# A 32x32 triangular solve by two 16x16 triangles and tensor products, in the first two of six attention blocks

## The chip, the cores and the metric

The kernel runs on one core of a Trainium2 chip. The metric is the device time of one execution in microseconds (us). Before the change it is 2233.88 us, the median of three runs (2229.7, 2233.88 and 2234.07). A core has a tensor engine (TensorE, PE in the profile), a vector engine (VectorE, DVE), a scalar engine (ScalarE, ACT), a general engine (GpSimd, POOL) and one that issues DMAs here (SyncE, SP). Each works through its own instructions in order, and waits for the others by semaphores.

## The reference

Three layers follow each other. The first is linear attention with the delta rule, one state per batch and head:

```
k_n = k / (norm(k) + 1e-6)
for t in range(768):
    y[t]  = q[t] @ state
    state = state + beta[t] * outer(k_n[t], v[t] - state^T k_n[t])
```

There are 4 batches of 8 heads, 768 tokens and a head size of 48. The second layer is `(h * tanh(softplus(h))) @ w_out` with `h = x @ w_in`, over 3072 tokens, model size 384 and inner size 2048. The third has a gate that is normalised eight times over rows and columns (all tokens enter every column sum), and eight experts of inner size 1024, whose outputs are added with the gate's weights.

## The kernel before

The attention is computed by chunks of 64 tokens, two chunks to a block, six blocks. Inside a chunk the token loop becomes a unit lower triangular system, one per batch, head and chunk: 64 systems of 64x64 in a block. The matrix is the masked product of the keys with themselves (tile `gx`, written by `st_g` and `mask_g`). A system is cut in two triangles of 32x32 and a square. `lane_in_one` transposes `gx` in 32x32 squares, so that each partition of tile `lane` holds one 32x32 triangle, with 1 on its diagonal. `elim_ops` inverts all of them by 30 steps on VectorE; a step multiplies a row into a column (into scratch in `t11`) and adds it (60 operations in all, L1083 and L1089). `st_lane_out` transposes the result back into `t11` (L1098) and into `diag`, which lies in tile `yd` (L1099). Then TensorE forms the square's part: `st_m1` (L1126, on `t11`), `st_place`, `st_m2` (L1141, on `diag`). After that come the block's chain of stages: `st_w` (L1190), `st_s` (L1208, L1209), `st_z` (L1168, L1169), `st_y` (L1224), each with a pass of VectorE or ScalarE behind it, and `st_x1`, which turns the block's output for the second layer.

Block 0 stands alone at the start (the prologue): nothing else for TensorE is there but the keys' products of block 1 (`st_g(1, ...)`, L1020 and L1021, raw values that ScalarE copies out; GpSimd masks them later) and the masked products of queries and keys (`gq`, L1006, four pairs of VectorE operations). Block 1's elimination begins there with 18 operations on GpSimd (`elim1`).

Window 0 follows: 16 steps of the second layer on block 0's tokens. A step `f` does `m_first(f)` on TensorE (nine products, L300), Mish on ScalarE, `gl` on VectorE (L1299), and two steps later `m_second(f)` (nine products, L1310). In window 0 the weights also come in and are split into parts: `begin_decode`, three integer passes on VectorE (L189, L192, L197) and one more (L262), after ScalarE's conversions (L206, L260). Steps with the experts follow in the same window (`hl` and L324). Beside the steps a table, `PLACES`, names the marks (s0 to s15, f1 to f4, s16 to s23) at which the next block's stages are put in: the first number `m0` is the mark at which what is left of the elimination is drained and transposed back; the list behind it places the chain. `fill(x)` hands out waiting elimination operations worth x us by the planner's own cost at the end of each step. So the order of every engine is fixed when the program is built.

Of the kernel before, what the change touches and what calls it, by code (L numbers as in the profile page):

```python
# [84 lines left out]
def delta_mish_sinkhorn_kernel(  # L85
# [240 lines left out]


    gate = const.tile([128, 192], F32, name="gate")
    sk = {}
    for name, at, cols in (("ones", 0, 128), ("m", 128, 3), ("cs", 136, E), ("cr", 144, E), ("rs", 152, NT)):  # L330
        sk[name] = gate[:, at:at + cols]
# [445 lines left out]
    def o_store():  # L777

        u, half, t = todo.popleft()
        if t < 0:  # L780
            f, x, (n, d) = fin[u], slice(512 * half, 512 * half + 512), divmod(~t, KD)
            tt(out=f[:, d, x], in0=f[:, d, x], in1=f[:, 3 + 3 * n + d, x], op=ALU.add)
            return
            return True
        o_write(u, half, t, o_turn(u, half, t, (0, 1, 2)))

    todo = deque()
# [8 lines left out]
    if True:  # L796
# [9 lines left out]
        lane = ap_p.tile([128, 32, 32], F32, name="lane")  # L806
# [268 lines left out]
        def elim_ops(c, eng=(nc.vector,)):  # L1075
            ops = []
            for s in range(1, 31):
                n = 31 - s
                slot = [None]

                def prod(s=s, n=n, slot=slot):
                    slot[0] = t11.rearrange("p b i -> p (b i)")[:, 0:n * s].rearrange("p (n s) -> p n s", s=s)
                    eng[0].tensor_tensor(  # L1083
                        out=slot[0], in0=lane[:, s + 1:32, s:s + 1].to_broadcast([128, n, s]),
                        in1=lane[:, s:s + 1, 0:s].to_broadcast([128, n, s]), op=ALU.mult,
                    )
# [8 lines left out]
            return ops  # L1095

        def st_lane_out(c):
            nc.vector.transpose(out=t11.rearrange("p b i -> p i b"), in_=lane.rearrange("p t i -> p i t"))  # L1098
# [258 lines left out]
        with tc.manual_schedule():  # L1357
# [44 lines left out]
            for _, op in lane_in_one(0):  # L1402
                op()
            e0 = [op for _, op in elim_ops(0)]

            def el(n):
                for _ in range(n):
# [10 lines left out]
            banks[:] = [0, [A1, A1, (ps_o1, "o0")]]  # L1418
            for t in range(4):
                run(*[lambda hf=hf: st_g(1, t, hf, False) for hf in range(2)])  # L1420
            for n in range(4):
                begin_decode(n)
            el(len(e0) - 24)
            nc.vector.memset(mi_f[1][:, 0:1], 0.0)
            warm(12, i=1)
            el(len(e0))
            st_lane_out(0)

# [1 line left out]
                for _ in range(n):  # L1430
                    dq.popleft()[1]()

            def elim1(n, eng):
                elim_eng[0] = eng
                for _ in range(min(n, len(ops1))):
                    ops1.popleft()[1]()

            m1a = m_run(st_m1(0, 0, (32,)))
            m1a[0]()
            st_place(0, 0, (0, 2))  # L1440
# [2 lines left out]
            m2a()  # L1443
            m1b()
            wa = [st_w(0, t) for t in range(2)]
            for op in norm_ops(1, ALL):
                op()
            for t in range(4):
                prep_mb(1, t, nc.gpsimd)
            for t in range(4):  # L1450
                mask_g(1, t, nc.gpsimd)
            for p in wa:
                p()
            dec(1)
# [4 lines left out]
            for t in range(2, 4):  # L1459
                prep_v_act(0, t)  # L1460
            s0[0]()
            s0[1]()
            converts(1)
            z1 = [st_z(0, t) for t in range(2, 4)]
            z1[0]()
            gq[0]()
            z1[1]()
            gq[1]()
            run(*[lambda t=t: st_y(0, t) for t in range(2)])
            for n in range(4, 6):  # L1470
                fetch(n)
            for t in range(4):
                diag_left(1, t)
            in1 = [op for _, op in lane_in_one(1)]
            elim_eng = [nc.gpsimd]
            ops1 = deque(elim_ops(1, elim_eng))
            dec(2)
            wb = [st_w(0, t) for t in range(2, 4)]
            gq[2]()
            wb[0]()  # L1480
            gq[3]()
            wb[1]()
            run(*[lambda t=t: st_y(0, t) for t in range(2, 4)])
            for n in range(6, 8):
                fetch(n)
            decodes(2)
            converts(2)
            dec(2)
# [12 lines left out]
            elim_eng[0] = nc.vector  # L1501
            wslots.append(late_p.tile([128, 2, 2, DM], F32R, tag="e2", name=f"w{NS1 - 1}"))

        NU = U1 + U2
# [7 lines left out]
        def drain_decode():  # L1512
# [11 lines left out]
        def window(c):  # L1524

            pe = {m: [] for m in MARKS}
            rest = {m: [] for m in MARKS}
            late = {m: [] for m in MARKS}
            nxt, far = c + 1, c + 2
            if c < NE0:  # L1530
                for t in range(4):
                    rest[f"s{U1 + 1 + t}"].append(lambda t=t: logits(c, t))
            elif c > NE0:
                for t in range(4):
                    rest[f"s{1 + t}"].append(lambda t=t: logits(c - 1, t))
            if c == 0:
                for t in (2, 3):
                    pe["s1"].append(lambda t=t: st_s(0, t))
                rest["s3"].append(lambda: eq.extend(ops1))
                for t in range(4):  # L1540
                    rest[f"s{2 * t + 3}"].append(lambda t=t: prep_v(1, t))
                for i in range(8):
                    rest[MARKS[i + 8]].append(lambda t=i // 2, w=1 + i % 2: mask_p(1, t, (w,)))
            if nxt < NBLK:
                m0, at = PLACES[c][0:2]
                rest[MARKS[m0]].append(drain_elim)
                rest[MARKS[m0]].append(lambda: st_lane_out(nxt))
                for hf in range(2):
                    late[MARKS[m0 + 1]].append(lambda hf=hf: m_run(st_m1(nxt, hf))[0])
                    rest[MARKS[m0 + 2]].append(lambda hf=hf: st_place(nxt, hf, (0, 2)))  # L1550
                    late[MARKS[m0 + 2]].append(lambda hf=hf: m_run(st_m2(nxt, hf))[0])
# [24 lines left out]
            return pe, rest, late  # L1576

        with tc.manual_schedule():
            banks[:] = [0, [A1, A1]]
            for c in range(NBLK):  # L1580
# [36 lines left out]
                for f in range(U1 + (3 if c < NE0 else 2)):  # L1617
# [240 lines left out]
```

## Time and profile before

| | |
|---|---|
| median of three runs | 2233.88 us |
| profiled execution | 2229.53 us |
| its span in the trace | 2227.7 us |
| TensorE busy | 2165.4 us, 97% |
| VectorE busy | 1394.4 us, 63% |
| ScalarE busy | 691.9 us, 31% |
| GpSimd busy | 673.6 us, 30% |

The profiled execution is 1.8 us longer than its span, and 4.35 us shorter than the median. TensorE is busy nearly all the time as a whole. The change touches only the start, so the page's totals say little about it: the stretches that matter are the prologue (to about 79 us), the 16 steps of window 0 (79 to 182 us) and what is left of block 1's chain among the experts' steps (to 243 us). [...]

### The profile page before, as it was taken

The page shows a single profiled execution, that of the slowest core. Times are in us where ns is not written, and L with a number is a line of the kernel's source. Part 1 is how long each engine was busy: PE and PEld are TensorE (multiplying, and loading weights), DVE is VectorE, ACT ScalarE, POOL GpSimd, SP SyncE. Part 2 cuts the span into 40 slices and gives each one's busy share as a digit, 9 for nine tenths or more (in the row PEclk, how much of TensorE's full clock was granted, in tenths as well). Part 3 has the DMA queues.
Part 4 walks back from the last instruction along what each step waited for, and adds up shares of the span by engine and source line. Part 5 has one row for each costly group of instructions (what it writes and reads, how often), then busy time and mean ns, then how long its engine had stood idle before and what let it go on. Part 6 is the DMA issues. An engine that isn't in the chain of part 4 may idle for free.

```text
span 2227.7 us, 34746 instructions
## 1 busy us (share of the span) xinstructions
PE 2165.4 (97%) x14133; PEld 1792.0 (80%) x14133; DVE 1394.4 (63%) x2289; ACT 691.9 (31%) x1212; POOL 673.6 (30%) x528
## 2 busy tenths in 40 slices
PE   7889898999999999999999999999999999999999
PEld 6668787888888788888888888888888888888887
DVE  8894726473821276777776776666666666666665
ACT  6453332333324445233333322112212121211122
POOL 3504441435324656677878600000000000000000
PEclk7799999999999999999999999999999999999999
DMA  6576733544446446655555444444443454444441
GB/s 185 184 245 202 232 124 133 191 165 154 143 143 207 161 156 221 233 195 199 202 195 197 153 143 155 150 148 161 138 161 124 150 154 158 137 147 147 165 151 43
DMA packets 123648, 370.35 MB, mean 166 GB/s; under 512 B 9440, under 2 KB 51232, under 8 KB 123232
## 3 DMA queue, kind: packets, MB, share of 16 engines
q1 hardware_dynamic: 122912, 367.74, 48.3%
q8 instruction: 111, 1.82, 0.3%
q10 hardware_dynamic: 576, 0.39, 0.1%
q14 instruction: 49, 0.40, 0.1%
HBM read 274.15 MB, written 93.95 MB: 165 GB/s over the span
## 4 chain that ended last, share of the span: by engine, by line
PE 86%; DVE 8%; issue 2%; DMA 1%; POOL 1%; ACT 1%; SPq 0%; DVEq 0%; POOLq 0%; ACTq 0%
PE s L663 33%; PE b L596 31%; PE psh L300 7%; PE x L1310 6%; DVE t L1083 1%; DVE lane L1089 1%; PE y L324 1%; PE psa L1020 1%; DVE us L876 1%; PE psa L1168 1%; DVE lane L1053 1%; PE psa L1126 1%; PE psa L1141 1%; PE psa L1224 1%; PE psa L1190 1%
## 5 line engine op out<-in xcount | busy, mean ns | idle before, releaser
L596 PE MATMUL b<-gx,gw 128*128 128x512 f32 x3036 | 795.5, 390 | 0.1
L603 DVE TENSOR_TENSOR gt<-b,gt 128x512 f32<-128x512 f32 x644 | 436.0, 689 | 460.8 <-PE b L596 429.5
L596 PEld LDWEIGHTS b<-gx,gw 128*128 128x128 f32 x3036 | 568.5, 188 | 118.6 <-ACT gt L605 0.9
L663 PE MATMUL s<-gh,gw 128*128 128x512 f32 x2208 | 622.7, 390 | 0.6 <-DVE gy L706 0.4
L638 ACT ACTIVATE gh<-gt 128x512 fp32r<-128x512 f32 x368 | 232.8, 633 | 933.5 <-DVE gt L632 926.1
L663 PEld LDWEIGHTS s<-gh,gw 128*128 128x128 f32 x2208 | 413.6, 188 | 87.0 <-DVE gy L706 0.8
L663 PE MATMUL s<-gl,gw 128*128 128x512 f32 x1104 | 326.8, 390 | 0.0
L632 DVE SCALAR_TENSOR_TENSOR gt<-gt,gp 128x512 f32<-128x512 f32 x336 | 277.0, 825 | 4.5
L300 PE MATMUL psh<-x,w 128*128 128x512 f32 x1008 | 262.0, 405 | 11.8 <-DVE gl L1299 10.1
L663 PEld LDWEIGHTS s<-gl,gw 128*128 128x128 f32 x1104 | 206.8, 188 | 42.8
L300 PEld LDWEIGHTS psh<-x,w 128*128 128x128 f32 x1008 | 188.2, 192 | 59.8 <-DVE gl L1299 9.5
L641 POOL TENSOR_TENSOR gl<-gt,gh 128x512 fp32r<-128x512 f32 x128 | 186.3, 1462 | 77.4 <-ACT gh L638 72.3
L641 DVE TENSOR_TENSOR gl<-gt,gh 128x512 fp32r<-128x512 f32 x240 | 164.5, 686 | 37.0 <-ACT gh L638 36.8
L1299 POOL TENSOR_TENSOR gl<-x,gh 128x512 fp32r<-128x512 f32 x80 | 103.0, 1288 | 256.1 <-ACT gh L1297 238.5
L536 POOL TENSOR_TENSOR gx<-gxr,gx 128x768 fp32r<-128x768 f32 x18 | 33.3, 1847 | 407.0 <-ACT gx L535 407.0
L1310 PE MATMUL x<-gh,w 128*128 128x512 f32 x576 | 155.3, 406 | 0.0
L467 POOL TENSOR_TENSOR gw<-gr,gw 128x640 fp32r<-128x640 f32 x70 | 117.5, 1680 | 68.2 <-ACT gw L477 66.4
L1310 PEld LDWEIGHTS x<-gh,w 128*128 128x128 f32 x576 | 109.4, 194 | 24.0 <-issue 1.4
L1291 ACT ACTIVATE x<-psh 128x512 f32<-128x512 f32 x80 | 47.7, 596 | 132.3 <-PE psh L300 123.3
L1310 PE MATMUL x<-gl,w 128*128 128x512 f32 x288 | 82.8, 396 | 2.3 <-POOL gl L1299 2.3
L467 POOL TENSOR_TENSOR gw<-raw,gw 128x384 fp32r<-128x384 f32 x70 | 73.3, 1068 | 7.3 <-ACT gw L499 7.3
L984 POOL TENSOR_TENSOR kq<-kq,mask_sb 64x256 f32<-64x256 f32 (+1 forms) x72 | 58.6, 814 | 55.0 <-ACT kq L979 51.2
(203 smaller groups left out, 1984.8 us busy)
## 6 DMA issues: line engine op xcount, KB each, us to landing
gw<-wg SPq DMA_DIRECT2D x57, 1280.0 KB, 8.1
w<-wd SPq DMA_DIRECT2D x88, 768.0 KB, 4.4
gw<-wg SPq DMA_DIRECT2D x57, 768.0 KB, 5.1
wg<-gw SPq DMA_DIRECT2D x29, 1280.0 KB, 6.0
wg<-gw SPq DMA_DIRECT2D x29, 768.0 KB, 5.3
wd<-w SPq DMA_DIRECT2D x24, 768.0 KB, 5.7
gr<-in_w_dram SPq DMA_DIRECT2D x35, 384.0 KB, 3.2
raw<-in_w_dram SPq DMA_DIRECT2D x35, 384.0 KB, 3.8
```

What stands on the lines that cost most here:

```text
L300: mm(ps, lhsT=wi(u, pw, kc), rhs=(xh, xl)[px][:, kc, :], start=(n == 0), stop=(n == 3 * KD - 1))
L467: nc.gpsimd.tensor_tensor(out=w[:, 1, lo:hi], in0=r, in1=w[:, 0, lo:hi].bitcast(F32), op=ALU.subtract)
L596: mm(ps, lhsT=w[:, pw, i * 128:i * 128 + 128], rhs=x[:, px, j, :], start=(n == 0), stop=(n == last))
L603: add = lambda o, i: nc.vector.tensor_tensor(out=t[:, o], in0=ps, in1=t[:, i], op=ALU.add)
L632: nc.vector.scalar_tensor_tensor(out=t, in0=t, scalar=0.0, in1=pbs[u, e][:, o:o + 512], op0=ALU.max, op1=ALU.mult)
L638: nc.scalar.activation(out=h, in_=t, func=AF.Copy)
L641: return lambda: eng.tensor_tensor(out=l, in0=t, in1=h.bitcast(F32), op=ALU.subtract)
L663: mm(o[k], lhsT=w[:, pw, at:at + 128], rhs=hids[s, z][ph], start=(start and new and n == 0), stop=(end and not new and n == 2))
L984: nc.gpsimd.tensor_tensor(out=o, in0=o, in1=mask_sb[p, None, :].to_broadcast([64, hs.stop - hs.start, CH]), op=ALU.mult)
L1291: nc.scalar.activation(out=mi_x[u % 2], in_=hps.pop(u), func=AF.Mish)
L1299: eng.tensor_tensor(out=l, in0=p, in1=h.bitcast(F32), op=ALU.subtract)
L1310: mm(x2ps[c][k], lhsT=wo(u, pw, k * 128, k * 128 + 128), rhs=(h, l)[pg], start=(f == 0 and n == 0), stop=(f == U1 - 1 and n == 2))
```

## The change

For blocks 0 and 1 `half_ops` takes the place of `elim_ops`. It inverts the two 16x16 triangles on the diagonal of each 32x32 triangle at once (`lane2` addresses both, so `lanes` is a little longer), in 14 steps of two operations on VectorE with 28 to 112 elements each, after a `memset` on GpSimd that clears the square between them. The 16x16 square that is missing is then formed by TensorE: `st_e16` makes 128 products of 32x32 from the transposed result and `gx`, which ScalarE copies out through a mask (`low16`); `st_o16` makes 192 products of 32x16, added by VectorE to `t11` and `diag` (three operations per half). The other four blocks keep `elim_ops`.

In the prologue the four `gq` passes and the key norms of block 1 move up beside these products; the raw products of block 1 (`raw_g`), which stood before the end of the elimination, are spread between the stages of block 0's chain; the calls for the weights, the warm-up products (12 to 10) and block 1's copies `diag_left` move too. Block 1's part on GpSimd goes: all its 28 operations are put in at s11. `fill` hands out 0.6 us a step up to f = 11, then 3.4, in place of 1.2. `m0` goes from 11 to 13, the chain's marks by three, and `st_m1` and `st_m2` by a further one.

```
+            ops = [(0.0, lambda: nc.gpsimd.memset(lane[:, 16:32, 0:16], 0.0))]
+            for s in range(1, 15):
+                n = 15 - s
+                p = t[:, 0:2 * n * s].rearrange("p (k n s) -> p k n s", k=2, s=s)
...
+            for i in range(16):                                   # st_e16
+                t, h = 2 * hf + i // H, i % H
+                for p in range(0, 128, 32):
+                    o = p % 64
+                    mm(ps[p:p + 32, i], lhsT=g[p:p + 16, t, h, o:o + 32], rhs=t11[p:p + 16, t * H + h, :],
+                       start=True, stop=True)
+            return lambda: nc.scalar.activation(out=em(hf), in_=ps, func=AF.Copy, scale=low16)
...
+                for p in (0, 64):                                 # st_o16
+                    mm(ps[q, 0, i], lhsT=diag[q, b, :], rhs=e[q, i, 0:16], start=True, stop=True)
...
+                for p in range(0, 128, 32):
+                    mm(ps[q, 1, i], lhsT=e[q, i, :], rhs=diag[q, b, 16:32], start=True, stop=True)
...
-            el(len(e0) - 24)
+            raw_g((0, 0))
+            el(12)
             nc.vector.memset(mi_f[1][:, 0:1], 0.0)
-            warm(12, i=1)
+            warm(10, i=1)
             el(len(e0))
             st_lane_out(0)
+            ea, eb = st_e16(0, 0), st_e16(0, 1)
+            ea()
+            eb()
+            gq[0]()
+            oa, ob = st_o16(0, 0), st_o16(0, 1)
+            raw_g((0, 1))
...
-            for t in range(4):
-                mask_g(1, t, nc.gpsimd)
+            raw_g((1, 0), (1, 1))
             for p in wa:
                 p()
...
-            elim1(18, nc.gpsimd)
...
-            (11, two(14, 15, 17, 18, 19, 20, 21, 22), 16, [21, 22, 23, 24], two(23, 24, 25, 26), 18, 26, 26),
+            (13, two(17, 18, 19, 20, 21, 22, 23, 24), 16, [21, 22, 24, 25], two(23, 24, 25, 26), 18, 26, 26),
...
-                rest["s3"].append(lambda: eq.extend(ops1))
+                rest["s11"].append(lambda: eq.extend(half_ops(1)))
...
+                    if c == 0:
+                        late[MARKS[m0]].append(lambda hf=hf: st_e16(nxt, hf))
+                        late[MARKS[m0 + 1]].append(lambda hf=hf: st_o16(nxt, hf))
...
-                    fill(1.2 if not c else 3.2 if c >= NE0 and f > 8 else 2.0)
+                    fill((0.6 if f < 12 else 3.4) if not c else 3.2 if c >= NE0 and f > 8 else 2.0)
```

What this does to the order is seen at three places. The first is TensorE in the prologue, from the end of block 0's solve to the first stage of its chain. Before, `st_m1` (written from `t` and `gx`) comes directly behind the warm-up products, all raw products of block 1 (`kq_144` to `kq_147`) lie ahead of it, so that the rows run:

```order
L1020 MATMUL psa<-kq_147 64x2x64
L1021 MATMUL psa<-kq_147 64x2x64
L1345 LDWEIGHTS f_185
L1345 MATMUL spare<-f_185 128x512
...
L1126 MATMUL psa<-t_167,gx_152 32x32 x34
L1141 MATMUL psa<-yd,mb_176 32x32 x2
...
L1141 MATMUL psa<-yd,mb_176 32x32 x2
L1190 MATMUL psa<-r,gx_152 64x48 x32
L1141 MATMUL psa<-yd,mb_177 32x32 x32
L1208 MATMUL psa<-us_162,kt_148 48x48
```

Now the new products (L1129 for `st_e16`, L1140 and L1145 for `st_o16`) come first, then half of block 1's first raw products, then `st_m1` (L1186) and `st_m2` (L1201):

```order
L1405 MATMUL spare<-f_185 128x512
L1129 MATMUL psa<-t_167,gx_152 32x32 x128
L1140 MATMUL psa<-mb_176,yd 32x16 x32
L1145 MATMUL psa<-yd,mb_176 32x16 x64
L1140 MATMUL psa<-mb_177,yd 32x16 x32
L1145 MATMUL psa<-yd,mb_177 32x16 x64
L1022 MATMUL psa<-kq_144 64x2x64
...
L1186 MATMUL psa<-t_167,gx_152 32x32 x34
L1201 MATMUL psa<-yd,mb_176 32x32 x2
...
L1250 MATMUL psa<-r,gx_152 64x48 x32
L1022 MATMUL psa<-kq_145 64x2x64
...
L1201 MATMUL psa<-yd,mb_177 32x32 x32
```

Two of the eight parts of the raw products (`kq_145`) now lie between `st_w` (on `r`) and the second half of `st_m2`, and four more stand behind the stages `st_s` and `st_y`, where before there were none.

The second place is VectorE around the end of block 1's solve in window 0. Before, two or three elimination operations stand in each step up to this place; the drain's 22 follow the `gl` of step 10 (L1299), and the transposes back come behind them:

```order
L189 TENSOR_SCALAR kq_141<-kq_141 128x768
L192 SCALAR_TENSOR_TENSOR kq_141<-kq_141 128x768
L197 SCALAR_TENSOR_TENSOR kq_141<-kq_141 128x768
L262 TENSOR_TENSOR w_89<-kq_140,w_89 128x768
L1299 TENSOR_TENSOR gl<-psh,gh 128x512
L1083 TENSOR_TENSOR t_167<-lane 128x198
L1089 TENSOR_TENSOR lane<-lane,t_167 128x9x22
...
L1098 STREAM_TRANSPOSE t_167<-lane 128x32x32
L1099 STREAM_TRANSPOSE yd<-lane 128x32x32
```

Now the rows begin with the `gl` of step 10, and no elimination stands ahead of it:

```order
L1359 TENSOR_TENSOR gl<-psh,gh 128x512
L1108 TENSOR_TENSOR t_167<-lane 128x28
L1115 TENSOR_TENSOR lane<-lane,t_167 128x2x14
L1108 TENSOR_TENSOR t_167<-lane 128x52
...
L262 TENSOR_TENSOR w_90<-kq_141,w_90 128x768
L1359 TENSOR_TENSOR gl<-psh,gh 128x512
L1115 TENSOR_TENSOR lane<-lane,t_167 128x2x13x2
...
L1359 TENSOR_TENSOR gl<-psh,gh 128x512
L1115 TENSOR_TENSOR lane<-lane,t_167 128x2x7x8
...
L1158 STREAM_TRANSPOSE t_167<-lane 128x32x32
L1159 STREAM_TRANSPOSE yd<-lane 128x32x32
```

Three operations have moved behind the `gl` of step 10, twelve behind that of step 11, and thirteen, with the transposes, behind that of step 12; a step's decoding stands between these groups.

The third place is TensorE in the same steps. Before, `st_m1` of block 1 (on `gx_153`) stands behind `m_first(12)` (weights `w_89`) and ahead of `m_second(10)` (L1310), and `st_m2` a step later:

```order
L300 MATMUL psh<-x_1107,w_89 128x512 x2
L300 MATMUL psh<-x_1108,w_89 128x512
L1126 MATMUL psa<-t_167,gx_153 32x32 x64
L1310 MATMUL x_1255<-gh,w_93 128x512
...
L300 MATMUL psh<-x_1107,w_90 128x512 x2
L300 MATMUL psh<-x_1108,w_90 128x512
L1141 MATMUL psa<-yd,mb_176 32x32 x32
L1141 MATMUL psa<-yd,mb_177 32x32 x32
L1310 MATMUL x_1255<-gh,w_1167 128x512
```

Now `m_first(13)` (weights `w_90`) is the last work ahead of block 1's products:

```order
L300 MATMUL psh<-x_1409,w_90 128x512 x2
L300 MATMUL psh<-x_1410,w_90 128x512
L1129 MATMUL psa<-t_167,gx_153 32x32 x128
L1370 MATMUL x_1539<-gh,w_1451 128x512
...
L300 MATMUL psh<-x_1409,w_91 128x512 x2
L300 MATMUL psh<-x_1410,w_91 128x512
L1140 MATMUL psa<-mb_176,yd 32x16 x32
L1145 MATMUL psa<-yd,mb_176 32x16 x64
L1140 MATMUL psa<-mb_177,yd 32x16 x32
L1145 MATMUL psa<-yd,mb_177 32x16 x64
...
L1186 MATMUL psa<-t_167,gx_153 32x32 x64
```

The products of `st_e16` stand where `st_m1` stood, but one step later; those of `st_o16` follow behind `m_first(14)`, `st_m1` behind `m_first(15)`, and `st_m2` a step behind that.

## Rows read from the trace of the kernel before

**Rows 1.** Windows: wall us, busy of PE, PEld, DVE, ACT, POOL; clock; DMA share; GB/s
```profile
43.87:58.62 14.75, 12.68 (x358) 12.03 (x355) 12.60 (x21) 9.82 (x27) 8.96 (x9) 0.50 0.01 3
58.62:62.03 3.41, 1.13 (x36) 1.00 (x33) 2.57 (x3) 0.81 (x1) 3.41 (x3) 1.00 0.02 5
62.03:79.10 17.07, 16.19 (x208) 14.51 (x209) 14.10 (x19) 7.58 (x16) 9.54 (x8) 0.50 0.60 189
...
98.90:141.00 42.10, 37.30 (x154) 28.18 (x152) 39.81 (x66) 22.89 (x32) 1.71 (x3) 0.99 0.83 281
141.00:147.36 6.36, 2.41 (x10) 1.61 (x9) 5.74 (x21) 2.12 (x4) 0.00 (x0) 1.00 1.00 404
147.36:157.60 10.24, 8.08 (x139) 7.08 (x140) 10.04 (x11) 4.20 (x7) 0.00 (x0) 0.50 0.30 91
...
182.00:198.80 16.80, 12.66 (x236) 11.05 (x234) 11.39 (x20) 6.42 (x12) 8.94 (x4) 0.80 0.41 94
198.80:243.30 44.50, 44.23 (x403) 39.48 (x403) 20.63 (x41) 14.70 (x30) 24.58 (x27) 1.00 0.65 244
```

**Rows 2.** What TensorE waited for, 17.8 to 79.1 us: total, times, longest
```profile
PE psa L1126 <- DVE t L1098: 2.9, 1, 2.9
PE psa L1224 <- DVE kq L1006: 2.7, 1, 2.7
```

**Rows 3.** Timeline of VectorE in block 0's elimination: start, duration, line, tiles
```profile
17.89 0.17 DVE L1083 TENSOR_TENSOR t<-lane 128x30 f32<-128x30 f32 x1
...
18.10 0.21 DVE L1089 TENSOR_TENSOR lane<-lane,t 128x30 f32<-128x30 f32 x1
...
38.00 0.27 DVE L1089 TENSOR_TENSOR lane<-lane,t 128x108 f32<-128x108 f32 x1
38.30 0.25 DVE L1083 TENSOR_TENSOR t<-lane 128x84 f32<-128x84 f32 x1
...
39.82 2.09 DVE L1098 STREAM_TRANSPOSE t<-lane 128x1024 f32<-128x1024 f32 x1
```

**Rows 4.** Timeline of TensorE: small products of blocks 0 and 1
```profile
46.21 0.24 PE L1126 MATMUL psa<-t,gx 32*32 32x32 f32 x2
...
46.26 0.24 PE L1126 MATMUL psa<-t,gx 32*32 32x32 f32 x2
...
149.52 3.63 PE L1126 MATMUL psa<-t,gx 32*32 32x32 f32 x128 [5.47 <-DVE t L1098]
...
210.00 0.27 PE L1020 MATMUL psa<-kq 48*64 48x128 f32 x1
...
210.11 0.27 PE L1020 MATMUL psa<-kq 48*64 48x128 f32 x1
```

**Rows 5.** Timeline of ScalarE and VectorE late in the prologue
```profile
61.66 1.40 DVE L1006 TENSOR_TENSOR kq<-psa,mask_sb 64x512 f32<-64x512 f32 x2
...
67.57 3.42 ACT L1061 ACTIVATE gx<-gx 32x256 f32<-32x256 f32 x8
```

**Rows 6.** Timeline of VectorE, then TensorE, one step of window 0
```profile
110.94 0.39 DVE L1083 TENSOR_TENSOR t<-lane 128x234 f32<-128x234 f32 x1
...
112.13 0.56 DVE L189 TENSOR_SCALAR kq<-kq 128x768 int32<-128x768 int32 x1
...
115.46 0.68 DVE L1299 TENSOR_TENSOR gl<-psh,gh 128x512 fp32r<-128x512 f32 x1
116.06 0.40 DVE L1089 TENSOR_TENSOR lane<-lane,t 128x238 f32<-128x238 f32 x1
...
111.08 2.35 PE L300 MATMUL psh<-x,w 128*128 128x512 f32 x9 [0.67 <-DVE gl L1299]
```

**Rows 7.** What TensorE waited for, 79.1 to 243.3 us
```profile
PE psh L300 <- DVE gl L1299: 10.1, 10, 4.4
PE psa L1126 <- DVE t L1098: 5.5, 1, 5.5
PE psa L1224 <- DVE us L876: 2.9, 1, 2.9
```

More of the change, by code (lines that the diff above doesn't have):

```diff
@@ L328, in delta_mish_sinkhorn_kernel @@
     gate = const.tile([128, 192], F32, name="gate")
+    low16 = gate[:, 132:133]
     sk = {}
@@ L805, in delta_mish_sinkhorn_kernel @@
         us = [[ap_p.tile([128, 2, DM], F32, name=f"us{g}{i}") for i in range(2)] for g in range(NG)]
-        lane = ap_p.tile([128, 32, 32], F32, name="lane")
+        lanes = ap_p.tile([128, 1056], F32, name="lane")
+        lane = lanes[:, 0:1024].rearrange("p (t i) -> p t i", i=32)
+        lane2 = lanes.rearrange("p (k m) -> p k m", k=2)[:, :, 0:512].rearrange("p k (t i) -> p k t i", i=32)
         t11 = ap_p.tile([128, 32, 32], F32, name="t11")
@@ L1095, in elim_ops, with half_ops, prod, add @@
             return ops
+        def half_ops(c):
+            t = t11.rearrange("p b i -> p (b i)")
+            ops = [(0.0, lambda: nc.gpsimd.memset(lane[:, 16:32, 0:16], 0.0))]
+            for s in range(1, 15):
+                n = 15 - s
+                p = t[:, 0:2 * n * s].rearrange("p (k n s) -> p k n s", k=2, s=s)
+                def prod(s=s, n=n, p=p):
+                    nc.vector.tensor_tensor(
+                        out=p, in0=lane2[:, :, s + 1:16, s:s + 1].to_broadcast([128, 2, n, s]),
+                        in1=lane2[:, :, s:s + 1, 0:s].to_broadcast([128, 2, n, s]), op=ALU.mult,
+                    )
+                def add(s=s, p=p):
+                    x = lane2[:, :, s + 1:16, 0:s]
+                    nc.vector.tensor_tensor(out=x, in0=x, in1=p, op=ALU.add)
+                cost = 0.2 + 2 * n * s / 960.0
+                ops += [(cost, prod), (cost, add)]
+            return ops
@@ new lines, in st_e16 @@
+        def st_e16(c, hf):
+            ps = bank().rearrange("p (b i) -> p b i", i=32)
+            g = gx(c)
+            for i in range(16):
[5 more added lines that the diff above has]
+            return lambda: nc.scalar.activation(out=em(hf), in_=ps, func=AF.Copy, scale=low16)
@@ new lines, in st_o16, with post @@
+        def st_o16(c, hf):
+            ps = bank().rearrange("p (w b i) -> p w b i", w=2, i=16)
+            e = em(hf)
+            for i in range(16):
+                b = 16 * hf + i
+                for p in (0, 64):
+                    q = slice(p, p + 32)
+                    mm(ps[q, 0, i], lhsT=diag[q, b, :], rhs=e[q, i, 0:16], start=True, stop=True)
+            for i in range(16):
+                b = 16 * hf + i
+                for p in range(0, 128, 32):
+                    q = slice(p, p + 32)
+                    mm(ps[q, 1, i], lhsT=e[q, i, :], rhs=diag[q, b, 16:32], start=True, stop=True)
+            bs = slice(16 * hf, 16 * hf + 16)
+            def post():
+                for p in (0, 64):
+                    x = t11[p:p + 32, bs, 0:16]
+                    vec.tensor_tensor(out=x, in0=x, in1=ps[p:p + 32, 0], op=ALU.add)
+                x = diag[:, bs, 16:32]
+                vec.tensor_tensor(out=x, in0=x, in1=ps[:, 1], op=ALU.add)
+            return post
@@ L1401, in delta_mish_sinkhorn_kernel @@
                 diag_left(0, t)
-            for _, op in lane_in_one(0):
-                op()
-            e0 = [op for _, op in elim_ops(0)]
+            in0 = [op for _, op in lane_in_one(0)]
+            e0 = [op for _, op in half_ops(0)]
+            for op in in0[0:2] + e0[0:1] + in0[2:]:
+                op()
+            e0 = e0[1:]
+            m = [mask_sb[:, x:x + 1] for x in (16, 32, 48)]
+            nc.gpsimd.tensor_tensor(out=low16, in0=m[1], in1=m[0], op=ALU.subtract)
+            nc.gpsimd.tensor_tensor(out=low16, in0=low16, in1=m[2], op=ALU.subtract)
+            nc.gpsimd.tensor_scalar(out=low16, in0=low16, scalar1=1.0, scalar2=None, op0=ALU.add)
             def el(n):
@@ L1417, in delta_mish_sinkhorn_kernel, with raw_g @@
             gq = [st_gq(0, t, True) for t in range(4)]
-            banks[:] = [0, [A1, A1, (ps_o1, "o0")]]
-            for t in range(4):
-                run(*[lambda hf=hf: st_g(1, t, hf, False) for hf in range(2)])
-            for n in range(4):
-                begin_decode(n)
-            el(len(e0) - 24)
+            CHAIN, SIDE = [A1, A1], [(ps_o1, "o0")]
+            def raw_g(*parts):
+                banks[:] = [0, SIDE]
+                for t, hf in parts:
+                    st_g(1, t, hf, False)()
+                banks[:] = [0, CHAIN]
+            raw_g((0, 0))
+            el(12)
             nc.vector.memset(mi_f[1][:, 0:1], 0.0)
-            warm(12, i=1)
+            warm(10, i=1)
             el(len(e0))
@@ L1431, in dec @@
                     dq.popleft()[1]()
[L1433 to L1436, printed above, removed]
+            banks[:] = [0, CHAIN]
+            ea, eb = st_e16(0, 0), st_e16(0, 1)
[3 more added lines that the diff above has]
+            oa, ob = st_o16(0, 0), st_o16(0, 1)
+            SIDE = [(ps_o1, "o0"), (ps_h, "h"), (ps_h, "h")]
+            CHAIN = [A1, A1, (ps_o1, "o1"), (ps_o1, "o2")]
+            raw_g((0, 1))
+            for op in norm_ops(1, ALL):
+                op()
+            for t in range(4):
+                prep_mb(1, t, nc.gpsimd)
+            gq[1]()
+            gq[2]()
+            begin_decode(0)
+            begin_decode(1)
+            oa()
+            gq[3]()
+            ob()
             m1a = m_run(st_m1(0, 0, (32,)))
@@ L1445, in delta_mish_sinkhorn_kernel @@
             wa = [st_w(0, t) for t in range(2)]
[L1446 to L1450, printed above, removed]
-                mask_g(1, t, nc.gpsimd)
+            raw_g((1, 0), (1, 1))
             for p in wa:
@@ L1458, in delta_mish_sinkhorn_kernel @@
             m2b[0]()
-            for t in range(2, 4):
-                prep_v_act(0, t)
+            raw_g((2, 0), (2, 1))
+            prep_v_act(0, 2)
             s0[0]()
             s0[1]()
-            converts(1)
             z1 = [st_z(0, t) for t in range(2, 4)]
             z1[0]()
-            gq[0]()
+            converts(1)
+            prep_v_act(0, 3)
             z1[1]()
-            gq[1]()
             run(*[lambda t=t: st_y(0, t) for t in range(2)])
             for n in range(4, 6):
+                fetch(n)
+            raw_g((3, 0), (3, 1))
+            for t in range(4):
+                mask_g(1, t, nc.gpsimd)
+            begin_decode(2)
+            begin_decode(3)
+            dec(2)
+            wb = [st_w(0, t) for t in range(2, 4)]
+            wb[0]()
+            wb[1]()
+            run(*[lambda t=t: st_y(0, t) for t in range(2, 4)])
+            for n in range(6, 8):
                 fetch(n)
@@ L1474, in delta_mish_sinkhorn_kernel @@
             in1 = [op for _, op in lane_in_one(1)]
[L1475 to L1485, printed above, removed]
             decodes(2)
```

9 lines of the change are left out of this document (4 added, 5 removed).

## The prediction

> **What bounds the kernel now.** TensorE is busy 97% of the span, so the kernel can gain only where TensorE waits or runs at half clock, and loses whatever work TensorE is given on top. I read the windows first, then what TensorE waited for, then the timelines of the places that these name. Both early stretches that the change touches are exceptions to the 97%. In the prologue TensorE runs at 0.50 of its clock from 43.87 to 58.62 and from 62.03 to 79.10 us, with 12.68 of 14.75 and 16.19 of 17.07 us busy; in between it is at 1.00 but busy for 1.13 of 3.41 us [rows 1]. It waits 2.9 us for block 0's transposed result and 2.7 us for the masked `gq` [rows 2]. In the steps of window 0 VectorE is busy 39.81 of 42.10 us, TensorE 37.30 [rows 1]: VectorE paces them. From 79.1 to 243.3 us TensorE waits 10.1 us in ten times for `gl` (4.4 us of it once, early), 5.5 us for block 1's transposed result and 2.9 us for `us` in the chain [rows 7]. From 198.80 on it is busy 44.23 of 44.50 us [rows 1].
>
> **Prologue.** The 60 old operations run from 17.89 to 39.82 us, 21.9 us [rows 3]. The new 28 have 28 to 112 elements. Start to start, 30 elements take 0.21 us and 108 take 0.30 [rows 3]; on a line between these the sizes 28, 52, 72, 88, 100, 108 and 112, four times each, give 4 x (0.21 + 0.23 + 0.25 + 0.28 + 0.29 + 0.30 + 0.31) = 7.5 us. So the result is transposed at about 25.5 in place of 39.8, and ready for TensorE at 27.6.
>
> 14.3 us are saved there, but most of it is spent at once. `st_e16` is 128 products of 32x32. The nearest row is the first products of block 0, mixed from four corners of the array: two of them follow the same pair after 0.05 us at half clock, 27 ns each [rows 4], so 3.4 us. ScalarE's copy is some 0.6 (half as many elements take 3.42 / 8 = 0.43 [rows 5]). `st_o16` has 64 products of 32x16 on two corners and 128 on four. Block 1's `st_m1`, 64 products in 3.63 us at half clock (the trace shows two records for each), is 57 ns for each [rows 4]. With the price of 32 columns `st_o16` takes 64 x 57 + 128 x 27 ns = 7.1 us, with half of it 3.6. I take the first, since each product still loads its own weights. Half a raw part more, 1.8, and `st_m1` starts at 27.6 + 3.4 + 0.6 + 7.1 + 1.8 = 40.5 at the latest. VectorE meanwhile does the second transpose (2 us), four `gq` pairs of 1.40 [rows 5], the norms (some 1) and six additions of 256 elements (0.47 each by the same line, 2.8), and is there at about 39. Before, `st_m1` starts at 42.06, behind the transpose that starts at 39.82 and lasts 2.09 with its signal [rows 3]: a gain of 1.5 to 3; I take 2.5.
>
> Then six of the eight raw parts stand in the chain, which before lay beside the elimination and cost nothing. Two products start every 0.11 us at full clock [rows 4]; a part has eight such pairs, 0.9 us, or 1.8 at half clock. Six are 5.3 to 10.6 us. The chain's idle time up to 79.10 is 2.07 + 2.28 + 0.88 = 5.2 us [rows 1], and they may fill it. At half clock 5.4 us are left over, at full clock nothing. ScalarE's `diag_left` copies, 3.42 us [rows 5], now stand right ahead of the copies that start window 0: between nothing and 3.4. With the clock at half in most of it, I take -2.5 + 4.2 + 0.3, **+2 us** for the prologue, with bounds of -8 (raw parts hidden, part of the chain at full clock) and +7.
>
> **Steps of window 0.** Between two `gl` VectorE takes 5.12 us in the shown step, 1.19 of it elimination (110.94 to 112.13) [rows 6]. Without that it needs 3.93. TensorE's share of the step is 5.12 less its wait of 0.67, so 4.45: it becomes the bound, and the step saves the 0.67 and no more. The nine short waits make 10.1 - 4.4 = 5.7 us [rows 7]; of the long one I count 0.8, since GpSimd's 18 operations beside it go. **-6.5 us**, bounds -10 and -3. The transfers don't hold this up: 281 GB/s over 42.10 us in eight steps are 1.48 MB a step, and the DMA engines moved 404 GB/s when full [rows 1], 3.7 us. But 4.45 asks for 332 GB/s, and that is the reason for the upper bound.
>
> **The solve of block 1.** All 28 operations now stand behind three `gl`, each with a full step's decoding between. From the `gl` of step 11 it is 0.60 us to the next operation [rows 6], twelve elimination operations at 0.21 to 0.31 (3.4), decoding 3.33 (112.13 to 115.46) [rows 6], `gl` 0.60, thirteen operations (3.5), and the transpose of 2.09 [rows 3]: 13.5 us until TensorE may start `st_e16`. It has only `m_first(13)` to do, which starts behind the same `gl` and lasts 2.35 [rows 6]; everything else is queued behind `st_e16`. That is a wait of 13.5 - 0.6 - 2.35 = 10.5 in place of 5.47 [rows 4]: **+5 us**, bounds +2 and +7. No reason in the trace lets it shrink below the old one, unless the planner's steps run ahead.
>
> **The products of block 1** are plain additional work for TensorE, in a stretch where it has no more waits to hide them. The clock is at 0.50 from 147.36 to 157.60, behind the stall [rows 1], and the stall stays, so `st_e16` again costs 3.4. `st_o16` comes a step later; at full clock it is half of the above, 3.5 or 1.8. **+6.9 us**, bounds 3.5 (all at full clock, half price) and 10.5 (all at half clock). [...]
>
> **The chain of block 1** stands three marks later, and one more for `st_m1`. Before, it waits 2.9 us for `us` between 182.00 and 198.80, where TensorE is busy only 12.66 of 16.80 us [rows 1, 7]. Those stages now lie beside the last steps and the experts. That can hide the waits (-3) or set them between experts' steps, each with VectorE's pass behind `hl` (+6). I take **+2**.
>
> **Sum:** 2 - 6.5 + 5 + 6.9 + 2 = +9.4 us on the profiled execution, 2229.5 (its span of 2227.7 and 1.8 around it), which lies 4.4 under the median. On the median of 2233.9 it is 2243.3. From about 300 us on the order is the same as before, so what is lost here stays.
>
> **Rivals.** [...] *No change:* the steps gain their 10 us, the products cost the lower 3.5, and the chain's waits hide: 2 - 10 + 5 + 3.5 - 1 = -0.5, 2233. For it: the steps' idle time is real. Against: 4.45 us of TensorE's own work in a step. *Worse:* the products at 10.5, the raw parts exposed (+7), and the chain between the experts (+6), with steps that gain only 5: +23, 2257. Here the wait for `gl` would be replaced by waits for `us` and `r`.
>
> **How the numbers follow.** The forecast, 2243 with its own range of 2238 to 2252, has 0.47; the full-clock prologue 0.2, no change 0.2, worse 0.13. Such a measurement can tell 0.2%, 4.5 us, from no change. Faster by more than that has 0.26 (the first rival's, and a little of the second), within it 0.2, slower 0.54. The range reaches from 2226 to 2256.
>
> **What would show it.** In the profile after: VectorE's elimination of block 0 takes about 7.5 us and `st_m1` starts near 40; `m_first(0)` not before 79 us; steps of about 4.4 us with TensorE waiting under 0.2 for `gl`; one wait of TensorE of about 10 us for the transpose of block 1, followed by half clock; the products of `st_o16` in about 3.5 us. I am wrong if the prologue's clock is at 1.00 and window 0 starts before 74, if that wait stays near 5, or if `st_e16` and `st_o16` together take under 4 us.

## The result, and the profile after

The changed kernel takes 2257.24 us (median of four runs, 2255.67 to 2260.0) where the kernel before takes 2231.79 beside it: the ratio is 1.0116, with an interval of 1.0098 to 1.0134, 25.4 us slower. The forecast was 2243 with a range up to 2256. The direction was right and the size was not: +9.4 us were forecast. The profiled execution has a span of 2254.8 us against 2227.7.

Starts of the same work in the two traces show where the time went:

| start of | before, us | after, us | difference |
|---|---|---|---|
| `st_m1` of block 0 | 42.06 | 50.10 | +8.0 |
| `gl` of step 0 | 85.37 | 98.20 | +12.8 |
| `gl` of step 10 | 140.98 | 146.67 | +5.7 |
| `gl` of step 15 | 176.69 | 196.82 | +20.1 |
| `hl` of the first expert step | 198.80 | 222.81 | +24.0 |
| `hl` of the last expert step | 242.73 | 271.03 | +28.3 |

Two stretches lose, each where the new products stand; the steps between them gain. What TensorE waited for in the profile after, from 17 to 260 us (engine, tile and line, releaser: total, times, longest), answers to [rows 2, 7]:

```profile
PE psa L1129 <- DVE t L1158: 11.8, 2, 10.5
PE psa L1129 <- issue: 6.2, 2, 4.9
PE psa L1140 <- issue: 5.1, 2, 3.0
PE psh L300 <- DVE gl L1359: 4.3, 2, 4.0
PE psa L1145 <- issue: 4.0, 3, 1.6
```

The wait for `gl` has gone from 10.1 us in ten times to 4.3 in two. The wait for the transpose is one of 10.5 us in place of 5.5. But there are 15.3 us of a kind of which the kernel before has 0.7 in this stretch: TensorE stands inside the new products (L1129 is `st_e16`, L1140 and L1145 are `st_o16`) and waits for "issue", that is, for no other engine and no transfer of data that this view shows. The timeline of TensorE in the prologue after shows where:

```profile
28.31 1.75 PE L1129 MATMUL psa<-t,gx 16*32 16x32 f32 x176 [1.25 <-DVE t L1158]
34.99 1.29 PE L1129 MATMUL psa<-t,gx 16*32 16x32 f32 x80 [4.93 <-issue]
36.08 1.44 PE L1140 MATMUL psa<-mb,yd 32*32 32x16 f32 x47
39.68 0.56 PE L1140 MATMUL psa<-mb,yd 32*32 32x16 f32 x14 [2.17 <-issue]
...
40.11 1.68 PE L1145 MATMUL psa<-yd,mb 32*32 32x16 f32 x109
43.14 0.42 PE L1145 MATMUL psa<-yd,mb 32*32 32x16 f32 x17 [1.35 <-issue]
43.38 1.81 PE L1140 MATMUL psa<-mb,yd 32*32 32x16 f32 x61
...
46.97 1.30 PE L1145 MATMUL psa<-yd,mb 32*32 32x16 f32 x81 [1.07 <-issue]
...
50.10 2.02 PE L1186 MATMUL psa<-t,gx 32*32 32x32 f32 x68
```

Each product leaves two records. The first stop, of 4.93 us, comes after 176 records. Between it and the next lie 80 + 47, and then, with the single records that are left out here, 128 and 128: TensorE stops after every 64 products, whichever stage they belong to. Products and stops take from 28.31 to 48.27, 20.0 us, 9.5 of them in four stops. In block 1 it is the same:

```profile
164.82 2.03 PE L1129 MATMUL psa<-t,gx 16*32 16x32 f32 x134 [10.55 <-DVE t L1158]
168.15 1.86 PE L1129 MATMUL psa<-t,gx 16*32 16x32 f32 x122 [1.29 <-issue]
169.94 2.93 PE L1370 MATMUL x<-gh,w 128*128 128x512 f32 x6
...
175.79 1.15 PE L1140 MATMUL psa<-mb,yd 32*32 32x16 f32 x61
...
176.82 1.21 PE L1145 MATMUL psa<-yd,mb 32*32 32x16 f32 x124
...
181.82 0.45 PE L1140 MATMUL psa<-mb,yd 32*32 32x16 f32 x9 [2.95 <-issue]
...
182.14 1.78 PE L1145 MATMUL psa<-yd,mb 32*32 32x16 f32 x114
185.55 0.40 PE L1145 MATMUL psa<-yd,mb 32*32 32x16 f32 x12 [1.63 <-issue]
185.88 2.93 PE L1370 MATMUL x<-gh,w 128*128 128x512 f32 x6
...
192.24 2.21 PE L1186 MATMUL psa<-t,gx 32*32 32x32 f32 x128
```

`st_e16` takes 5.1 us there, `st_o16` 10.1, 15.2 in all, with stops of 1.29, 2.95 and 1.63. The DMA queues of the stretch with the longest stop, 28 to 42 us (queue, kind: packets, MB, share of 16 engines), say what may be missing:

```profile
q1 hardware_dynamic: 2457, 3.50, 70.4%
q8 instruction: 3, 0.05, 1.4%
```

The queue that is called "instruction" moves blocks of 0.05 MB / 3, some 16 KB. In the whole execution it has 1.98 MB in 121 packets after the change and 1.82 in 111 before; the ten blocks more, over the 640 new products, are one for 64. That is the distance of the stops. The theory, then (A): TensorE runs out of code (the instructions themselves, which by this theory are what these blocks bring), since tiny products use it up faster than it is brought in. The rivals: the array itself is slow with such small tiles (B), or the products are slow only in what stands around them here.

When the blocks come speaks for A. From 40.7 to 41.8 us nothing but one block moves:

```profile
q8 instruction: 1, 0.02, 5.5%
```

It starts at 40.81 and takes 0.96 us, and the stop of 1.35 us ends at 43.14. The four blocks that move beside block 0's products have landed at 33.6, 38.2, 41.8 and 45.8 us, and the four stops end at 34.99, 39.68, 43.14 and 46.97, 1.2 to 1.5 us behind them; in block 1 it is 1.2 to 1.4 behind each of three. At the longest stop the block doesn't start to move before 32.50, 4.2 us after the first product, while the DMA engines are full (share 1.07).

### The profile page after: what moved, and what is told of

It reads as the page before. It is cut to its first block, busy times and chain, and to the rows that moved or that the text cites. A ratio compares the mean times of both kernels' runs of the same rounds, so it can differ in the third digit from the quotient of the medians.

```text
span 2254.8 us, 37257 instructions
## 1 busy us (share of the span) xinstructions
PE 2173.6 (96%) x15411; PEld 1799.2 (80%) x15411; DVE 1375.9 (61%) x2255; ACT 694.2 (31%) x1216; POOL 659.9 (29%) x515
## 3 DMA queue, kind: packets, MB, share of 16 engines
q8 instruction: 121, 1.98, 0.3%
## 4 chain that ended last, share of the span: by engine, by line
PE 86%; DVE 6%; issue 1%; DMA 1%; POOL 1%; ACT 1%; SPq 0%; DVEq 0%; ACTq 0%; POOLq 0%
PE s L664 33%; PE b L597 30%; PE psh L300 8%; PE x L1370 7%; PE psa L1022 1%; PE y L324 1%; PE psa L1284 1%; DVE t L1085 1%; PE psa L1228 1%; DVE lane L1091 1%; PE psa L1250 1%; DVE lane L1055 1%; DVE us L878 1%; DMA kq<-in_w_out_dram 1%; PE psa L1186 1%
```

## The experiments

**Each block by itself.** The first version keeps the prologue and block 0 of before:

```
-            e0 = [op for _, op in half_ops(0)]
+            e0 = [op for _, op in elim_ops(0)]
...          (prologue as before, without elim1)
```

> Only block 1 is solved the new way; the prologue and block 0 are as before. Theory A: TensorE runs out of code in the long runs of tiny products (each takes two weight loads and two multiplies); after some 64 to 120 products it gets only about 64 more per 3.5 us. Then block 1's 320 products cost about 15 us, and the kernel is 13 to 16 us slower than before (2245 to 2248), with 4 to 7 us of TensorE idle that the trace puts down to nothing. Theory B, the prediction's price of the products (27 to 57 ns each): 6 to 9 us slower (2238 to 2241).

Measured: 2246.19 us, ratio 1.0071 (1.0056 to 1.0086), +16 us. The second keeps block 1 of before:

```
+            for _ in range(18):
+                ops1.popleft()[1]()
...
-                rest["s11"].append(lambda: eq.extend(half_ops(1)))
+                rest["s3"].append(lambda: eq.extend(ops1))
...
-            (13, two(17, 18, 19, 20, 21, 22, 23, 24), 16, [21, 22, 24, 25],
+            (11, two(14, 15, 17, 18, 19, 20, 21, 22), 16, [21, 22, 23, 24],
```

> Only block 0 is solved the new way, with the prologue of the changed kernel; block 1 is as before. Theory A: st_m1 of block 0 starts near 50 us in place of 42, and the kernel is 11 to 14 us slower than before (2243 to 2246). Theory B: the products of block 0 are slow only because of what stands around them in the changed kernel; then 0 to 5 us slower (2232 to 2237).

Measured: 2244.39 us, 1.0060 (1.0045 to 1.0075), +14 us. Both blocks lose, each by about the time that theory A gives; together 30 us, 5 more than the whole change. (`st_m1` of block 0 starts at 52.1 us in the second, where about 50 was expected.) TensorE's issue waits inside the products are 6.7 us in the first and 8.9 in the second. That the products are slow because of what the other block does is out.

**As many products with half of the columns.**

```
-                    mm(ps[p:p + 32, i], lhsT=..., rhs=t11[p:p + 16, t * H + h, :],
+                    mm(ps[p:p + 32, i, 0:16], lhsT=..., rhs=t11[p:p + 16, t * H + h, 0:16],
...
-                    mm(ps[q, 0, i], lhsT=diag[q, b, :], rhs=e[q, i, 0:16], start=True, stop=True)
+                    mm(ps[q, 0, i, 0:8], lhsT=diag[q, b, :], rhs=e[q, i, 0:8], start=True, stop=True)
```

> The changed kernel with as many products, each with half of its columns (16 and 8 in place of 32 and 16; the other half of the result is left out, and the copies and additions are as much smaller). Theory A (code): time as the changed kernel within 3 us (2254 to 2258), the same idle time of TensorE inside the products. Theory B (the array, by columns): the 30 us in which the products stand shrink by 8 to 15, 2242 to 2249.

**Half as many products of twice the columns.**

```
-            for i in range(16):
+            for i in range(0, 16, 2):
...
-                    mm(ps[p:p + 32, i], lhsT=..., rhs=t11[p:p + 16, t * H + h, :],
+                    mm(ps[p:p + 32, i:i + 2], lhsT=..., rhs=t11[p:p + 16, t * H + h:t * H + h + 2, :],
```

> The changed kernel with half as many products, each twice as wide (64 and 32 columns), so as many columns in all; the values of every second product are not the right ones. Theory A (code): the idle time inside the products nearly goes, the products take 12 to 16 us less, 2240 to 2246. Theory B (the array, by columns): as the changed kernel within 3 us, 2254 to 2258.

With half of the columns (the other half of each result is left out) the kernel takes 2263.69 us, 6 more than the changed kernel and not less (33.6 us over the kernel before beside it, against 25.4); with half of the count 2244.09, 13 less. The version with half of the columns stops at the same places as the changed kernel, after the same records:

```profile
29.72 1.69 PE L1129 MATMUL psa<-t,gx 16*32 16x16 f32 x176
36.44 1.27 PE L1129 MATMUL psa<-t,gx 16*32 16x16 f32 x80 [5.03 <-issue]
37.53 1.42 PE L1140 MATMUL psa<-mb,yd 32*32 32x8 f32 x47
40.32 0.54 PE L1140 MATMUL psa<-mb,yd 32*32 32x8 f32 x14 [1.36 <-issue]
```

The durations of the pieces are the same too (1.69 us for 176 records of half the width, 1.75 above): the columns don't set the pace even between the stops. The version with half of the count has half the products between 29.14 and 41.74, and `st_m1` starts 6.5 us earlier than in the changed kernel:

```profile
29.14 1.99 PE L1129 MATMUL psa<-t,gx 16*32 16x64 f32 x128
...
36.01 0.87 PE L1145 MATMUL psa<-yd,mb 32*32 32x32 f32 x49 [4.08 <-issue]
...
41.27 0.47 PE L1145 MATMUL psa<-yd,mb 32*32 32x32 f32 x17 [2.90 <-issue]
...
43.57 2.02 PE L1186 MATMUL psa<-t,gx 32*32 32x32 f32 x68
```

B is out, by columns at least: the cost goes with the number of products. Theory A's expectation that the stops nearly go was not met: 9.6 us in three of them are left in the fourth version, against 15.3 in seven. Why the third version is 6 us slower and not equal was not settled; 3 us of it are there by step 0, and the expected 2254 to 2258 was missed.

**Other transfers out of the way.** A small write holds back the loads until block 0's products are done:

```
-            for n in range(4):
+            for n in range(2):
                 fetch(n)
             nc.sync.dma_start(out=id_sb, in_=ident)
-            load_vt(1)
...          (behind ob())
+            nc.vector.memset(vt(1)[:, 0, 0:1], 0.0)
+            load_vt(1)
+            for n in range(2, 4):
...          (two such writes into bits(n))
+                fetch(n)
```

> The changed kernel, but the loads of block 1's values and of two of the four first weight parts wait until block 0's products are done (2.3 MB of the 3.5 MB that moved between 28 and 42 us). If the code for TensorE comes through the same DMA engines and stands in line behind these loads, the first stop inside block 0's products falls from 4.9 us to 1.3 to 2.5, as long as those of block 1, and st_m1 starts 3 to 4 us earlier; the kernel gains 1 to 4 us, less what the late loads cost (2253 to 2257). If the stop has its length whatever the transfers do, nothing changes there.

The timeline of TensorE in this version:

```profile
31.99 2.57 PE L1129 MATMUL psa<-t,gx 16*32 16x32 f32 x176 [3.32 <-DVE t L1158]
36.12 1.29 PE L1129 MATMUL psa<-t,gx 16*32 16x32 f32 x80 [1.56 <-issue]
...
39.73 0.55 PE L1140 MATMUL psa<-mb,yd 32*32 32x16 f32 x14 [1.09 <-issue]
...
43.45 0.41 PE L1145 MATMUL psa<-yd,mb 32*32 32x16 f32 x17 [1.62 <-issue]
...
47.01 1.30 PE L1145 MATMUL psa<-yd,mb 32*32 32x16 f32 x81 [0.80 <-issue]
...
50.14 2.02 PE L1186 MATMUL psa<-t,gx 32*32 32x32 f32 x68
```

The first stop is 1.56 us in place of 4.93, as the others, and from the first product to `st_m1` it is 18.15 us in place of 21.79. The block that ends it starts to move 1.5 us after the first product, in place of 4.2, and has landed 1.2 us before TensorE goes on. So this block does stand in line behind the loads, and stops remain with hardly any load: from 34.3 to 40 us, where those of 1.56 and 1.09 us lie, only some 16 KB start to move. The other versions agree: over all of them, the nine stops at a DMA share of 0.94 and more are 2.6 to 5.1 us long, and those at a share under 0.1 are 0.8 to 2.2.

`st_m1` does not start earlier, though, as was expected, but at 50.14 us against 50.10: in this profiled execution the elimination began 3.7 us later (the transpose in front of it at 20.01 against 16.32). That need not be the edit's doing: the two spread versions below have the same prologue, and their transposes behind the elimination start at 40.03 and 43.66. The whole kernel takes 2255.21 us, 1.0121 times the kernel before (1.0105 to 1.0138), where the changed one has 1.0116: no gain is shown. That the later loads take back what was won is likely and not shown.

**The products spread over the steps.** If code is the limit, the products should be cheap where large products, nine of which take 2.35 us [rows 6], stand between them. Prologue as before; block 1 by the new way, with its operations from step 1 and the products in four parts:

```
-                rest["s11"].append(lambda: eq.extend(half_ops(1)))
+                rest["s1"].append(lambda: eq.extend(half_ops(1)))
...
-                        late[MARKS[m0]].append(lambda hf=hf: st_e16(nxt, hf))
-                        late[MARKS[m0 + 1]].append(lambda hf=hf: st_o16(nxt, hf))
+                        late[MARKS[m0 + 1 + hf]].append(lambda hf=hf: st_e16(nxt, hf))
+                        late[MARKS[m0 + 3 + hf]].append(lambda hf=hf: st_o16(nxt, hf))
...
+            (8, two(15, 17, 18, 19, 20, 21, 22, 23), 16, [21, 22, 23, 24], ...
```

> Prologue and block 0 as before. Block 1 by two triangles, but its 28 operations stand in steps 1 to 8, the transposes in step 8, and the products a part in each step: 64, 64, 96, 96 in steps 9 to 12, with 18 large products between; st_m1 in step 13. Theory A (code): code is fetched during the large products, so TensorE's unexplained idle time is under 1 us in all, the 320 products cost 5 to 7 us, and there is no long wait for the transpose: 2 to 8 us faster than before (2222 to 2228). If a tiny product costs some 47 ns wherever it stands (15 us for 320): 1 to 5 us slower than before.

> As the spread version, all one step earlier and 15% more elimination in a step, so that st_m1, st_m2 and the chain of block 1 keep the marks of before. If the chain's later marks cost time (2 us in the prediction), this is 0 to 2 us faster than the spread version; theory A gives 2220 to 2228.

Measured: 2240.99 us (1.0052, 1.0036 to 1.0069) and 2241.67 (1.0055, 1.0040 to 1.0070): slower than before by 12 and 13 us, where 2 to 8 us faster was expected. In the first of the two the squares of block 2's keys take the buffers of `r` before `st_w` of block 1 reads them, which changes values and no amount of work. The products of `st_e16` did as theory A says, 1.28 and 1.29 us for 64. In the 96 of `st_o16` one stop was left, of 5.1 us in the first version and 4.3 in the second, at a DMA share of 0.94 and 0.98, where under 1 us was expected. The earlier chain of the second version shows no gain. And a new wait had come, 11.4 us of TensorE in step 1 of both. VectorE's timeline in the early one shows it:

```profile
94.07 0.68 DVE L1108 TENSOR_TENSOR t<-lane 128x28 f32<-128x28 f32 x1
94.78 0.77 DVE L1115 TENSOR_TENSOR lane<-lane,t 128x28 f32<-128x28 f32 x1
95.59 1.31 DVE L1108 TENSOR_TENSOR t<-lane 128x52 f32<-128x52 f32 x1
...
98.26 1.32 DVE L1108 TENSOR_TENSOR t<-lane 128x72 f32<-128x72 f32 x1
...
104.45 0.21 DVE L1115 TENSOR_TENSOR lane<-lane,t 128x72 f32<-128x72 f32 x1
104.69 0.25 DVE L1108 TENSOR_TENSOR t<-lane 128x88 f32<-128x88 f32 x1
```

Operations of 28 to 72 elements take 0.7 to 1.3 us up to 99.5 us, and those of 72 and 88 take 0.21 and 0.25 from 104 on. GpSimd multiplies from 89.47 to 103.10, from 92.73 on its masks, with operations of 0.8 to 2 us:

```profile
92.73 1.97 POOL L986 TENSOR_TENSOR kq<-kq,mask_sb 64x512 f32<-64x512 f32 x1
...
95.56 7.54 POOL L986 TENSOR_TENSOR kq<-kq,mask_sb 64x512 f32<-64x512 f32 x5
```

One by one, the two engines go in step: GpSimd's operations that start at 95.56, 96.90 and 98.23 take 1.25 or 1.26 us, and VectorE's three start 0.03 us behind them and take 1.30 to 1.32. All five slow ones end 0.05 to 0.09 us behind the operation of GpSimd beside them. So such an operation lasts here as long as what is left of its neighbour, whatever its own size.

**The same, behind GpSimd's work.** The operations start at step 4, and then, in a further version, `st_o16` stands in four parts:

```
-                rest["s1"].append(lambda: eq.extend(half_ops(1)))
+                rest["s4"].append(lambda: eq.extend(half_ops(1)))
...
+            (10, two(17, 18, 19, 20, 21, 22, 23, 24), 16, [21, 22, 24, 25], ...
...
-                    fill(1.0 if not c else ...
+                    fill(1.35 if not c else ...
...          (in the further version)
+                        late[MARKS[m0 + 3 + hf]].append(lambda hf=hf: st_o16(nxt, hf, 0))
+                        pe[MARKS[m0 + 4 + hf]].append(lambda hf=hf: st_o16(nxt, hf, 1))
```

> As the spread version, but block 1's 28 operations start at step 4 in place of step 1, the transposes stand in step 10, the products in steps 11 to 14, st_m1 in step 15, and the chain at the marks of the changed kernel. In the spread versions TensorE waited 11.4 us in step 1 while VectorE's small operations took 0.7 to 1.3 us each beside GpSimd's masks (0.2 without). If that neighbour is what made them slow, this wait goes, the operations take 0.2 to 0.3 us, and with one or two stops for code of 3 to 5 us the kernel is 2 to 10 us faster than before (2219 to 2228). If the products or the later chain cost more than theory A says, it is 0 to 8 us slower (2229 to 2237).

> As the one before, but the products of st_o16 stand in four parts of 48, before and behind the nine large products of a step, in place of two of 96. Theory A: the stop for code inside them (4 to 5 us in the spread versions, behind the 93rd product) shrinks to under 2 us, 1 to 4 us faster than the one before (2216 to 2226). If the stop has nothing to do with how many products stand together, no change against it.

Measured: 2236.33 us (1.0024, 1.0015 to 1.0033; 11 runs) and 2239.78 (1.0037, 1.0023 to 1.0051). The first is 5 us slower than before, the best of all versions with two triangles, where 2 to 10 faster was expected, or 0 to 8 slower if the products or the later chain cost more than theory A says; the second is not faster than it, against its expectation, with two stops of 1.2 and 1.3 us in place of one of 1.91. In the first, TensorE in block 1:

```profile
139.94 1.29 PE L1129 MATMUL psa<-t,gx 16*32 16x32 f32 x128
...
149.09 1.52 PE L1129 MATMUL psa<-t,gx 16*32 16x32 f32 x128
...
154.84 1.15 PE L1140 MATMUL psa<-mb,yd 32*32 32x16 f32 x61
...
165.41 0.31 PE L1145 MATMUL psa<-yd,mb 32*32 32x16 f32 x16 [1.91 <-issue]
...
171.57 2.21 PE L1186 MATMUL psa<-t,gx 32*32 32x32 f32 x128
```

The wait of 11.4 us is gone, and the small operations take 0.18 to 0.28 us. But with the elimination back in the steps TensorE waits for `gl` again, 13.0 us in eight times, one of 6.5, so that by the `gl` of step 15, at 176.16 us, this version is where the kernel before is, at 176.69, but `st_m1` has only just run and `st_m2` and the chain are to come. From there to the last `hl` it takes 74.2 us against 66.0, as the changed kernel does. None of the versions beats the kernel before.

## Why the prediction was wrong, step by step

The step that failed is **the price of the products**, in both places: "3.4 us" and "7.1 us" for block 0, "+6.9 us" for block 1. The mechanism of the forecast, added work on TensorE, was right; its size was not. Measured are 20.0 us from the first product to the last in block 0, where 11.1 were forecast with the copy, and 15.2 in block 1, where 6.9 were: 17 us more, and the sum was 16 short. That these two nearly agree is partly luck: below, other terms miss by some us either way. Less the stops it is 10.5 and 9.3, so the array's price was near in block 0 and 2.4 us too low in block 1; what was missing are the stops: once they begin, it is 3.5 to 4.7 us for 64 products from one to the next, by theory A because code has to be brought in. The experiments with half of the columns (6 us more) and half of the count (13 less) show that it is the number of products, the one with held loads (a first stop of 1.56 us in place of 4.93) that what they wait for stands in line with the loads. The rows that I took the price from hold at most 64 products [rows 4], as many as lie between two stops here, and no stop. "Issue" is among the waits of the kernel before as well, 0.7 us ahead of `st_w` in the prologue and two of them, 1.9 us together, for `st_m2` of later blocks, and I passed over it. Half clock comes on top: in `st_o16` of block 1, 124 records take 1.21 us ahead of the stop of 2.95 us, at a granted clock of 1.00, and 114 take 1.78 behind it, at 0.50.

**The prologue** was put at +2 and is +12.8: 8.0 by `st_m1`, where a gain of 2.5 was forecast, 8.9 of these 10.5 us by the products; and 4.8 behind that, where 4.5 were forecast for the raw products and the copies. The elimination ran as worked out: its 28 operations take 7.8 us (18.36 to 26.11), forecast were 7.5.

**The steps** were put at -6.5: from the `gl` of step 0 to that of step 10 it is 48.5 us in place of 55.6, -7.1. TensorE becomes the bound there: 35.60 us busy of 35.60, as the window shows, with steps of 3.9 to 4.6 and one of 5.9.

```profile
42.00:62.00 20.00, 12.29 (x452) 11.31 (x453) 10.81 (x15) 5.72 (x10) 7.15 (x7) 0.50 0.01 3
62.00:79.00 17.00, 15.29 (x376) 14.51 (x375) 9.60 (x15) 12.68 (x37) 5.03 (x4) 0.84 0.15 47
...
111.00:146.60 35.60, 35.60 (x156) 29.17 (x156) 31.79 (x41) 22.47 (x33) 0.00 (x0) 0.99 0.92 331
...
155.00:165.00 10.00, 0.17 (x13) 0.21 (x17) 9.41 (x21) 0.00 (x0) 0.00 (x0) 0.73 0.35 133
```

**The wait for the transpose** was put at 10.5 us and is 10.55, followed by half clock as forecast (granted 0.50 from 164.82 to 168.15). In the ten microseconds from 155 VectorE is busy 9.41 and TensorE 0.17.

**The chain** was put at +2. From the `gl` of step 15 to the last `hl` it takes 8.2 us more; 2.2 of these are `st_m2`, which stood ahead of that `gl` before. So 6.0, of the right sign, but as much as its worse case (+6). From the `gl` of step 10 to that of step 15 it takes 14.4 us more, 16.6 with `st_m2`; 11.9 were forecast for the longer wait and the products. That is 4.7 over, though the products alone are 8.3 over: `st_m1` took 2.21 us there in place of 3.63, and where the rest came back wasn't traced. No run takes the moved raw parts or the later chain by themselves.

**The rivals.** The full-clock prologue, which had 0.2, did not come. The full clock came late: from 42 to 62 us the granted clock is 0.50, and only behind that, with the raw products between the stages, 0.84 on the mean (windows above). What that gave back is not seen apart from the rest, and no run shows what a whole prologue at 1.00 would take. Of the "worse" case, 2257, the time was met by luck: the products cost more than its upper price, for another reason; the steps gained 7.1 and not 5; what stands behind `st_m1` in the prologue lost 4.8; only the chain's 6.0 is as that case has it. Nor is the array's own price what made the small products dear: where no stop stands, `st_e16` of the last version but one does 64 products, in 128 records, in 1.29 us at a granted clock of 1.00: 20 ns a product and 10 ns a record. The 27 ns at half clock [rows 4] are of a product of two records, so 13 a record.

## What to carry to other kernels

Count instructions, not only columns: a long run of products that took some 20 ns each stopped here after every 64, with 3.5 to 4.7 us from one stop to the next, by theory A because code came no faster. Behind busy DMA engines (share 1.07) the block came later yet, 4.2 us after the first product where it was 1.5 with the loads held back. Taking 32 operations of a block from VectorE (28 for 60) for 320 tiny matmuls saved 14 us of VectorE and cost 15 to 20 of TensorE. Spread between large matmuls, lots of 64 products cost 1.3 to 1.5 us each, but among lots of 96 each version still met a stop, of 1.9 to 5.1. And look at the waits that the profile calls "issue" before a change that adds instructions.

## What the runs showed of the hardware that was not expected

- In a long run of small products TensorE stopped after every 64 (128 records), by theory A for code. In the changed kernel the stops are 1.1 to 2.2 us long at a DMA share of 0.09 and less, and 2.95 and 4.93 where the DMA engines are full (share 1.01 and 1.07). The blocks of the queue called "instruction" have some 16 KB and take 0.9 to 1.2 us to move at these stops, and TensorE goes on 1.2 to 1.5 us after one has landed.
- Between the stops, with the clock at 0.94 to 1.00, a product from four corners takes 20 ns (1.28 us for 64), and the width of 32 or 16 columns makes little difference (1.75 and 1.69 us for 88 of them).
- A VectorE operation of 28 to 72 elements took 0.7 to 1.3 us while GpSimd multiplied, and some 0.2 us without. The longest started and ended with a GpSimd operation of 1.26 us, so here it is the neighbour's length that counts; the decoding passes of 768 elements took 1.90 against 0.96 us.
